# A gated linear recurrence and a gated feed-forward layer on one core: half-wide first gate units, weights read by 32 partitions, and early transfers issued by GpSimd

## The chip, the cores and the metric

The kernel runs on one core of a Trainium2 chip. A core has engines that run side by side and wait for each other by semaphores: TensorE (matrix products, with a separate step that loads the stationary operand), VectorE, ScalarE, GpSimd, and SyncE, which here only issues transfers. Transfers are carried out by 16 DMA engines. The metric is the time of one execution on the device, in microseconds; lower is better. The three timed executions of the kernel before gave 872.43, 873.46 and 875.8 us, so the time before is 873.46 us.

## The reference, cut to what matters

```python
# attention: B, H, S, D = 4, 8, 768, 48
mag = sqrt(a_re**2 + a_im**2)
scale = minimum(mag, 0.999) / (mag + 1e-06)
a = (a_re + 1j * a_im) * scale             # one complex gate per feature and step
for t in range(S):
    state = a[t] * state + outer(k[t], v[t])   # state: D x D per head, kept as re and im
    y[t] = q[t] @ state.real

# feed-forward, on x = y with heads side by side: 3072 rows of 384 features, inner width 1536
rms = sqrt(mean(x * x) + 1e-06)
xn = x / rms * rms_g
out = (silu(xn @ w_gate) * (xn @ w_val)) @ w_out
```

The three weights come as 64-bit floats and must be made 32-bit floats on the chip.

## The kernel before

The 768 steps of each of the four batches are cut into chunks of 128 rows, 24 in all. Within a chunk the recurrence is a masked product of rotated and scaled keys and queries; between chunks a state is carried. Gates are worked on in *units* of two chunks (256 rows): magnitudes, running products, arctangents, running sums of angles, sines and cosines, and then the rotation of k and q. The rotated rows are moved by transfers into the layout that TensorE needs (`kr`, `qr`).

The program is written in lanes of steps. A small scheduler (`Order`) gives each step an estimated duration and picks the next step by estimated time when the program is built; this fixes the order of the instructions on every engine. On the chip each engine goes through its own list in order.

```python
def load_gates():
    for u in range(NU):                       # NU = 12 units of UC = 2 chunks
        ...
        for name, ap in (("re", a_re), ("im", a_im)):
            aside = u == 0 and name == "im"   # ScalarE issues the first im, SyncE the rest
            yield step("ACT" if aside else "SP", 0.0 if aside else 3 * order.ISSUE, ...)

def gates():
    n1 = ND * T                               # 768 elements per partition
    ...
    for u in range(NU):
        ...                                   # squares, roots, magnitudes (ScalarE, VectorE)
        yield E("ACT", ac_us(n1), [K("tan")], lambda: act_(out=im, in_=im, func=AF.Arctan), table=["atan"])
        ...                                   # running products, running sums, sine, cosine
        for i, (o, x, f) in enumerate((("ks", "k", s), ("k", "k", y), ("qs", "q", s), ("q", "q", y))):
            ...                               # rotations: rot0 .. rot3

def move_rows():                              # moves of the rotated rows, all issued by SyncE
    ...
            def move(i, t=t, two=two):
                name, rows = ("kr", "qr")[i // 2], (1 - i % 2) * D
                ...
                for j in range(ND):
                    nc.sync.dma_start(out=two[name][rows + j * L:rows + (j + 1) * L],
                                      in_=t[("ks", "k", "qs", "q")[i]][:, j])
    ...                                       # dec, decay: the chunk's decay by way of HBM

def rows_of(ap, j):                           # how a third of a gate or value weight is read
    return ap.rearrange("(p j l) f -> j p l f", j=ND, l=32)[j]

# raw weights: 18 pieces of 0.79 MB; the first EARLY = 4 have buffers of their own,
# the others share two
def fetch():
    ...
                for j in range(ND):
                    nc.sync.dma_start(out=to[:, j], in_=rows_of(ap[:, f:f + n], j))

def narrow():                                 # 64-bit floats to 32-bit ones, four steps a piece
    for i, (to, ap, _, _) in enumerate(parts):
        ...
        yield step("ACT", 0.05 + ac_us(n), [("raw", i)], share, ends=[("share", i)])
        yield step("DVE", tt_us(n), [("raw", i), ("piece", i - 2) if i > 1 else None], shifted)
        yield step("DVE", tt_us(n), [("share", i)], signed, ends=[("both", i)])
        yield step("POOL", 1.6, [("both", i)], total, ends=[("piece", i)])

def scores():
    for n in range(N):                        # N = 24 chunks
        ...                                   # s_ps = kr.T @ qr per head (TensorE), mask (VectorE)
        ...                                   # kt_ps: keys turned (TensorE), kt copied (ScalarE)

def finish():
    ...                                       # state_ps, the carried state, y_ps

def feed_forward(groups):
    for g in groups:                          # 12 groups of two chunks
        for f in range(NF):                   # 12 tiles of the inner width
            ...                               # gv_ps: gate and value product (TensorE)
            ...                               # silu (ScalarE), times value into hT (VectorE)
        for i in range(UC):
            for part in range(2):             # out_ps: half an output each (TensorE)
                ...
```

Between `y_ps` and the feed-forward product stand the row norm: squares on ScalarE, a sum on TensorE (`ss_ps`), a power on GpSimd, a spread on TensorE, and `xT` on VectorE.

Of the kernel before, what the change touches and what calls it, by code (L numbers as in the profile page):

```python
# [28 lines left out]
P = 128  # L29
C = 128  # L30
# [15 lines left out]
class Order:  # L46
# [11 lines left out]
    RATE = 0.2  # L58

    def __init__(self):  # L60
        self.clock, self.ends, self.lanes, self.table, self.moved = {}, {}, [], None, 0.0
        self.free = {}
# [4 lines left out]
    def begin(self, step, late):  # L67
# [10 lines left out]
        return at + late, at  # L78

    def run(self):  # L80
        while self.lanes:
# [19 lines left out]
            lane[2] = None  # L101
            emit()
# [3 lines left out]
            if switch:  # L106
                self.table = more["table"][0]
            self.clock[engine] = end = at + us + switch
            if "mb" in more:
                self.moved = max(self.moved, at + 0.4) + more["mb"] / self.RATE  # L110
                end = self.moved + self.LAND
# [438 lines left out]
def fast(tc, ctx, qT, kT, v, a_re, a_im, w_gate, w_val, w_out, rms_g, out, H, bad):  # L550
# [12 lines left out]
    NU = N // UC  # L563
# [13 lines left out]
    EARLY = 4  # L577
    first = ExitStack()
    early = first.enter_context(tc.tile_pool(name="early", bufs=EARLY))
    pools = {}  # L580
# [15 lines left out]

    def columns(x, j, odd, p):


        at = 128 * p + (0, 32 + 16 * odd, 80)[j]  # L600
        return x.rearrange("p h d -> p (h d)")[:, at:at + 32]

    def rows_of(ap, j):

        return ap.rearrange("(p j l) f -> j p l f", j=ND, l=32)[j]
# [21 lines left out]
    starts = filled("starts", [P, ND, UC, C], 0.0)  # L627
# [8 lines left out]
    ends = consts.tile([P, NU, ND, UC], FP32, name="ends")  # L636
    range_ = consts.tile([P, NU], FP32, name="range_")
# [7 lines left out]
    gcol = consts.tile([P, ND], FP32, name="gcol")  # L645

# [3 lines left out]
    UN = [dict() for _ in range(NU)]  # L650
    U = [dict() for _ in range(N)]


    def load_gates():
        for u in range(NU):
            b, c = divmod(u * UC, NCH)
            t = UN[u]

            def gate(name, ap, queue, t=t, b=b, c=c):
                t[name] = prep.tile([P, ND, T], FP32, tag=name, name=name, bufs=2)  # L660
                rows = ap[b].rearrange("(h j l) s -> j l h s", j=ND, l=L)
                for j in range(ND):
                    queue.dma_start(out=t[name][:, j], in_=rows[j][:, :, c * C:c * C + T])

            for name, ap in (("re", a_re), ("im", a_im)):
                aside = u == 0 and name == "im"
                yield step("ACT" if aside else "SP", 0.0 if aside else 3 * order.ISSUE,
                           [("moved3", u - 2) if u > 1 else None],
                           lambda name=name, ap=ap, q=nc.scalar if aside else nc.sync: gate(name, ap, q),
                           mb=0.39, ends=[(name, u)])  # L670

    def load_rows():
        for u in range(NU):
            t = UN[u]

            def rows(name, ap, t=t, u=u):
                t[name] = prep.tile([P, ND, T], FP32, tag=name, name=name)
# [516 lines left out]
```

## Time and profile before

The profile follows one execution of 872.1 us.

| engine | busy us | share of the span |
|---|---|---|
| TensorE, products | 748.0 | 86% |
| TensorE, weight loads | 608.4 | 70% |
| VectorE | 414.2 | 47% |
| ScalarE | 352.4 | 40% |
| GpSimd | 57.7 | 7% |

| group of instructions | count | busy us | mean ns |
|---|---|---|---|
| up-projection, gate and value (two rows) | 1728 | 428.1 | 388 and 381 |
| output product | 576 | 194.7 | 491 |
| scores | 384 | 61.6 | 326 |
| state | 320 | 35.0 | 269 |
| VectorE, gate operation over 768 elements | 12 each | 11.4 to 13.0 | 948 to 1083 |
| ScalarE, gate operation over 768 elements | 12 each | 9.9 to 11.2 | 828 to 933 |
| GpSimd, last step of a weight's conversion | 18 | 35.8 | about 1990 |

A product of 32-bit floats is two instructions in these counts. TensorE's matmuls overlap each other, so a busy share near 100% means only that it has no gap. In the slices of the page each digit is a tenth of one fortieth of the span (21.8 us). The chain that ended last is 64% TensorE and 13% transfers. 75.24 of the 76.46 MB that are moved go through one queue, SyncE's; ScalarE's carries 0.39 MB, and no data transfer is issued by GpSimd.

### The profile page before, as it was taken

How to read it: one execution, taken by the hardware profiler on the slowest of the kernel's cores; microseconds unless marked ns; L12 is line 12 of the kernel's file. 1: busy time of each engine (PE TensorE's matmuls, PEld its weight loads, DVE VectorE, ACT ScalarE, POOL GpSimd, SP SyncE). 2: the span in 40 equal slices, each digit the busy share in tenths (PEclk: the TensorE clock that was granted, in tenths of full speed). 3: DMA queues.
4: the chain of work that ended last, by engine and by line, in shares of the span. 5: the costliest groups of instructions: out<-in, count | busy, mean ns of one | idle time of the engine just before them, and what ended most of it. 6: DMA issues, size and time to landing. Idle time of an engine off the chain costs nothing.

```text
span 872.1 us, 11793 instructions
## 1 busy us (share of the span) xinstructions
PE 748.0 (86%) x4770; PEld 608.4 (70%) x4770; DVE 414.2 (47%) x684; ACT 352.4 (40%) x544; POOL 57.7 (7%) x66
## 2 busy tenths in 40 slices
PE   0008848769788989999999999999999999999997
PEld 0007647668565778878787788877788778886784
DVE  5636537658677776765845664212211222311120
ACT  6525436546566766776743663110111111110010
POOL 2210102101121000000000000000000000000000
PEclk9999957979889999999999999999999999999999
DMA  5345544674837936666318370008400026200420
GB/s 154 102 87 145 107 91 139 100 169 99 153 97 111 146 101 95 110 123 84 82 30 111 81 108 1 0 11 110 155 0 1 1 66 189 72 1 23 159 73 22
DMA packets 98330, 76.46 MB, mean 88 GB/s; under 512 B 36828, under 2 KB 85980, under 8 KB 98268
## 3 DMA queue, kind: packets, MB, share of 16 engines
q1 hardware_dynamic: 97836, 75.24, 41.1%
q8 instruction: 39, 0.64, 0.3%
q10 hardware_dynamic: 432, 0.39, 0.2%
q14 instruction: 23, 0.19, 0.1%
HBM read 51.98 MB, written 4.76 MB: 65 GB/s over the span
## 4 chain that ended last, share of the span: by engine, by line
PE 64%; DMA 13%; DVE 5%; ACT 3%; SPq 2%; issue 1%; POOL 0%; DVEq 0%; ACTq 0%
PE gv_ps L1072 33%; PE out_ps L1096 18%; PE y_ps L996 3%; PE s_ps L927 3%; PE state_ps L967 3%; DMA dec<-ends 3%; DMA kr<-k 3%; DMA qr<-qs 2%; DMA raw<-in_w_val_dram 2%; SPq L800 1%; PE ss_ps L1019 1%; PE kt_ps L946 1%; DMA kr<-ks 1%; DMA raw<-in_w_out_dram 1%; DVE k L589 1%
## 5 line engine op out<-in xcount | busy, mean ns | idle before, releaser
L1072 PE MATMUL gv_ps<-xT,wg 128*128 128x256 f32 x864 | 216.9, 388 | 2.7 <-DVE xT L592 1.5
L1072 PE MATMUL gv_ps<-xT,wv 128*128 128x256 f32 x864 | 211.2, 381 | 1.2 <-POOL wv L885 1.2
L1096 PE MATMUL out_ps<-wo,hT 128*128 128x384 f32 x576 | 194.7, 491 | 1.4 <-POOL wo L885 1.3
L1072 PEld LDWEIGHTS gv_ps<-xT,wg 128*128 128x128 f32 x864 | 165.1, 194 | 28.3 <-issue 2.4
L1072 PEld LDWEIGHTS gv_ps<-xT,wv 128*128 128x128 f32 x864 | 165.3, 191 | 24.4 <-POOL wv L885 1.6
L589 DVE TENSOR_TENSOR hT<-gv_ps,hT 128x256 f32<-128x256 f32 x144 | 59.9, 422 | 218.3 <-ACT hT L1076 218.2
L1096 PEld LDWEIGHTS out_ps<-wo,hT 128*128 128x128 f32 x576 | 107.5, 191 | 70.8 <-POOL wo L885 2.7
L1076 ACT ACTIVATE hT<-gv_ps 128x256 f32<-128x256 f32 x144 | 54.2, 383 | 209.6 <-PE gv_ps L1072 209.2
L927 PE MATMUL s_ps<-qr,kr 96*128 96x128 f32 x384 | 61.6, 326 | 86.9 <-DMA dec<-ends 67.8
L927 PEld LDWEIGHTS s_ps<-qr,kr 96*128 96x128 f32 x384 | 57.0, 235 | 89.5 <-issue 87.6
L1029 POOL TENSOR_TENSOR rs<-ssq,mhalf 128x1 f32<-128x1 f32 x24 | 17.1, 714 | 571.3 <-DVE ssq L1024 570.4
L1105 ACT COPY ot<-out_ps 128x384 f32<-128x384 f32 x24 | 11.3, 477 | 93.0 <-PE out_ps L1096 93.0
L967 PE MATMUL state_ps<-vz,kt 128*96 128x48 f32 x320 | 35.0, 269 | 15.3 <-ACT kt L950 15.3
L967 PEld LDWEIGHTS state_ps<-vz,kt 128*96 128x96 f32 x320 | 34.4, 187 | 19.0 <-ACT kt L950 16.3
L592 DVE SCALAR_TENSOR_TENSOR xT<-y_ps,gcol,rb 128x128 f32<-128x128 f32 x72 | 20.9, 344 | 38.5 <-ACT rb L1037 25.6
L932 DVE TENSOR_TENSOR am<-s_ps,causal 128x512 f32<-128x512 f32 x48 | 32.1, 684 | 9.0 <-PE s_ps L927 8.4
L905 DVE TENSOR_REDUCE least__115<-raw 128x1 f32<-128x768 f32 x18 | 17.0, 945 | 31.0 <-DMA raw<-in_w_out_dram 16.3
L1076 ACT ACT_TABLE_LOAD x24 | 30.8, 1283 | 0.4
L950 ACT COPY kt<-kt_ps 128x384 f32<-128x384 f32 x40 | 17.5, 479 | 33.3 <-PE kt_ps L946 33.3
L996 PE MATMUL y_ps<-am,vz 128*32 128x128 f32 x768 | 29.2, 299 | 0.0
L589 DVE TENSOR_TENSOR sz<-state_ps,sz 96x384 f32<-96x384 f32 x16 | 8.8, 550 | 40.0 <-PE state_ps L967 39.9
L996 PEld LDWEIGHTS y_ps<-am,vz 128*32 128x32 f32 x768 | 21.9, 119 | 4.9 <-issue 3.3
(97 smaller groups left out, 731.0 us busy)
## 6 DMA issues: line engine op xcount, KB each, us to landing
raw<-in_w_out_dram SPq DMA_DIRECT2D x12, 768.0 KB
re<-in_a_re_dram SPq DMA_DIRECT2D x36, 128.0 KB
k<-in_k_dram SPq DMA_DIRECT2D x24, 192.0 KB
q<-in_q_dram SPq DMA_DIRECT2D x24, 192.0 KB
vz<-in_v_dram SPq DMA_DIRECT2D x24, 192.0 KB
raw<-in_w_gate_dram SPq DMA_DIRECT2D x18, 256.0 KB
raw<-in_w_val_dram SPq DMA_DIRECT2D x18, 256.0 KB
kr<-ks SPq DMA_DIRECT2D x36, 128.0 KB
```

Of the source, the lines that this page charges most:

```text
L589: nc.vector.tensor_tensor(out=o, in0=x, in1=y, op=op)
L592: nc.vector.scalar_tensor_tensor(out=o, in0=x, scalar=c, in1=y, op0=op0, op1=op1, **kw)
L905: nc.vector.tensor_reduce(out=least_[:, i:i + 1], in_=words(raws.pop(i))[1].bitcast(FP32), axis=mybir.AxisListType.X, op=ALU.min, apply_ab ...
L927: nc.tensor.matmul(u["s_ps"][a][:, h], lhsT=u["k"][:, a * HH + h], rhs=u["q"][:, a * HH + h], start=True, stop=True)
L932: nc.vector.tensor_tensor(out=u["am"][a], in0=u["s_ps"][a], op=ALU.mult, in1=causal.unsqueeze(1).to_broadcast([C, HH, C]))
L950: nc.scalar.copy(out=u["kt"][a], in_=u["kt_ps"][a])
L967: nc.tensor.matmul(u["st_ps"][:, h], lhsT=u["kt"][h // HH][:, h % HH], rhs=u["v"][:, h, 0:D], start=True, stop=True)
L996: nc.tensor.matmul(u["y_ps"][32 * p:32 * (p + 1), j], lhsT=columns(left, j, odd, p), rhs=right(h), start=side == 0 and i == 0, stop=side = ...
L1029: nc.gpsimd.tensor_tensor(out=u["rs"], in0=u["ssq"], in1=mhalf, op=ALU.pow)
L1072: nc.tensor.matmul(ps[:, i], lhsT=w_[:, f * P // FW, d, cols], rhs=t["xT"][:, d], start=d == 0, stop=d == ND - 1)
L1076: nc.scalar.activation(out=t["hT"][:, f], in_=t["gv", f][:, 0], func=AF.Silu)
L1096: nc.tensor.matmul(t["o_ps", i], lhsT=t["hT"][:, f, i * C:(i + 1) * C], rhs=wo[:, f], start=f == 0, stop=f == NF - 1)
```

## The change: what it does and what it is for

1. **Half-wide first units.** The first unit of two chunks is split into two units of one chunk. Their operations cover 384 elements instead of 768, so that the first chunk's rows can be rotated before the second chunk's are done.
2. **Where raw weights land.** The four buffers for early raw weights are gone. The first four pieces land in the buffers `hT` of the feed-forward layer, which are not needed until later, and the others in two buffers `raw2` and in one half of `hT`.
3. **By 32 partitions.** A raw gate or value weight is read in four transfers of 32 partitions with three runs each, instead of three transfers of 128 partitions. The gain `rms_g` is read in the same manner.
4. **Who issues.** GpSimd issues the first six raw weights and, for the first two units, the moves of `qs` and `q`. ScalarE issues `im` for both half units.
5. **Fillers.** Where the scheduler expects TensorE to stand idle before a product that starts a stage, it places products of two constants (`ident`, `causal`) into the tile that the stage overwrites anyway. They are to keep TensorE's clock up.
6. **The scheduler.** It knows a slow state of TensorE, two transfer queues, and that GpSimd's sum holds VectorE; conversions of weights are held back until the first rotations are placed.

The listed order of the instructions changes accordingly: chunks 0 and 1 are interleaved on VectorE and ScalarE without a weight between them; TensorE does all twelve up-projection tiles of group 0 and one half output before chunk 2's scores, where before six tiles stood; ten fillers stand before the first scores and ten before chunk 2's.

```diff
+    units = [(0, 1), (1, 1)] + [(n, UC) for n in range(2, N, UC)]
+    NU = len(units)
...
+    def busy(ps):
+        n = ps.shape[1] // C
+        for _ in range(int((order.gap - 0.3) / (n * 0.215))):
+            nc.tensor.matmul(ps, lhsT=ident[:, 0:ps.shape[0]], start=True, stop=True,
+                             rhs=causal.unsqueeze(1).to_broadcast([C, n, C]))
...
-    def rows_of(ap, j):
-        return ap.rearrange("(p j l) f -> j p l f", j=ND, l=32)[j]
+    def rows_of(ap, p):
+        return ap.rearrange("(p j l) f -> p l j f", j=ND, l=32)[p]
...
+    hT = [consts.tile([P, NF, T], FP32, name="hT%d" % i) for i in range(2)]
+    raw2 = [consts.tile([P, ND, 2 * FW], I32, name="raw%d" % i) for i in range(2)]
...
-                aside = u == 0 and name == "im"
+                aside = u < 2 and name == "im"
...
             def move(...):
+                queue = nc.gpsimd if u < 2 and i > 1 else nc.sync
...
-                    nc.sync.dma_start(out=two[name][rows + j * L:rows + (j + 1) * L],
+                    queue.dma_start(out=two[name][rows + j * L:rows + (j + 1) * L],
...
+    EARLY = 6
+    def room(i):
+        two = (0, 1) if i < 2 else (2, 3) if i < 2 * NW and i % 4 > 1 else (4, 5)
...
+            aside = i < EARLY
+            queue = nc.gpsimd if aside else nc.sync
...
-                for j in range(ND):
-                    nc.sync.dma_start(out=to[:, j], in_=rows_of(ap[:, f:f + n], j))
+                for p in range(H // 2):
+                    queue.dma_start(out=to[32 * p:32 * (p + 1)], in_=rows_of(ap[:, f:f + n], p))
...
-            yield step("POOL", 1.6, [("both", i)], total, ends=[("piece", i)])
+            more = dict(late=lambda i=i: (0.05 if i < 2 * NW else 0.3) if ("rot", 1) in order.ends else LATE)
+            yield step("POOL", 2.3, [("both", i)], total, ends=[("piece", i)], holds=("DVE", 1.2))
...
             def pairs(u=u):
                 for a in range(2):
                     u["s_ps"].append(ps_a.tile([C, HH, C], FP32, tag="a", name="s_ps"))
+                    if a == 0:
+                        busy(flat(u["s_ps"][a]))
...
-    order.lane(gates(), 0.1)
+    order.lane(gates([0]), 0.05)
+    order.lane(gates(range(1, NU)), 0.1)
```

## The prediction, made before the changed kernel had run

> **What bounds the kernel now.** I read the page's forty slices first, then cut the span into stages where the slices change, then asked who TensorE waits for, then read the transfers of the first stage. The slices (TensorE's busy tenths, its granted clock, the DMA engines, GB/s):
>
> ```profile
> PE   0008848769788989999999999999999999999997
> PEclk9999957979889999999999999999999999999999
> DMA  5345544674837936666318370008400026200420
> ```
>
> TensorE does nothing in three slices, is ragged and partly at a low clock up to about slice 14, and is full afterwards. The table by stage (TensorE busy, weight loads, VectorE, ScalarE, GpSimd, then clock, DMA share, GB/s):
>
> ```profile
> 0.00:63.60 63.60, 0.00 (x0) 0.03 (x1) 32.93 (x39) 29.13 (x35) 14.03 (x28) 1.00 0.48 118
> 63.60:116.00 52.40, 37.58 (x264) 33.25 (x264) 29.87 (x51) 27.68 (x39) 6.53 (x5) 0.89 0.52 114
> 116.00:174.00 58.00, 44.68 (x321) 39.84 (x321) 35.92 (x57) 27.18 (x39) 9.02 (x6) 0.76 0.51 116
> 174.00:310.00 136.00, 112.11 (x847) 90.45 (x848) 98.52 (x149) 85.39 (x119) 18.53 (x12) 0.88 0.66 124
> 310.00:865.50 555.50, 553.51 (x3341) 444.83 (x3340) 216.78 (x392) 182.49 (x314) 9.60 (x15) 1.00 0.33 70
> ```
>
> From 310 us on TensorE is 99.6% busy at full clock: nothing can be won there except by arriving with more work done. Before 310 us it stands still for 63.6 us, then loses 246.4 - 194.4 = 52 us to gaps, and runs part of the rest at the low clock. What it waits for, up to 310 us (total, times, longest):
>
> ```profile
> PE s_ps L927 <- DMA dec<-ends: 67.8, 3, 63.6
> PE s_ps L927 <- DMA qr<-q: 17.3, 3, 9.2
> PE state_ps L967 <- ACT kt L950: 15.3, 3, 7.2
> ```
>
> These are rotated rows that arrive late, and a copy on ScalarE. The chain behind that copy leads to a raw weight: before the state product at 129.15 stand a transfer of 9.37 us (118.37) and the conversion behind it in ScalarE's order. Why are transfers slow? SyncE's issues, and the DMA from 20 to 40 us:
>
> ```profile
> 20.85 8.22 SPq L853 DMA_DIRECT2D raw<-in_w_gate_dram  x3
> 29.12 7.62 SPq L853 DMA_DIRECT2D raw<-in_w_val_dram  x3
> 36.84 3.76 SPq L800 DMA_DIRECT2D kr<-ks  x3
> ...
> DMA  2222222222222222222222222222222222222223
> GB/s 106 98 98 102 106 98 102 98 98 98 98 98 102 102 98 98 98 102 98 98 98 102 98 98 98 98 106 98 98 98 98 98 102 98 98 98 98 102 98 117
> ```
>
> A quarter of the engines works, at a constant 98 GB/s; issues that take 1.9 us for three elsewhere take 8. The first rotated rows were ready on VectorE at 31.6 us but were issued at 36.84, and the last landed only at 63.6.
>
> **The Trainium skill.** "DMA: Bandwidth & Descriptors", section "Why a DMA increments its semaphore by 16 and not by 1", says that the number of engines is the largest k up to 16 dividing the slowest dimension of both patterns. Gate and value weights are read as p=4, l=32: k is 4, and 98 GB/s on a share of 0.26 agrees. With l=32 outermost k is 16. "TensorE: Matmul & The Clock Gate", Part 1, says that the array's clock halves after an idle window of some 3.4 us and comes back after as long a busy one. The trace agrees: the first eight score products take 3.75 us at 63.6 and 1.85 us at 320.71. "SBUF — State Buffer", "Who interferes with whom", says that a VectorE instruction with two SBUF inputs blocks against a GpSimd one that reads SBUF. Agrees: a product of 0.95 us took 2.46 at 27.36 beside GpSimd's weight sum (26.54 to 29.0). The DMA page's "Latency and other measured facts" gives GpSimd's transfers about 1 us to the first byte; no transfer in this trace is issued there, so this is the figure I know least.
>
> **TensorE's work, which stays.** Warm durations from the chain: an up-projection tile 2.59 us (276 instructions in 59.57), half an output 3.87 (84 in 27.09), scores 1.85, transposes 0.66, state 1.32, y 1.89 with a state and 0.90 without, sums 0.66, spread 0.22. Work: 144 x 2.59 = 373.0; 48 x 3.87 = 185.8; 24 x 1.85 = 44.4; 20 x 0.66 = 13.2; 20 x 1.32 = 26.4; 20 x 1.89 + 4 x 0.90 = 41.4; 24 x 0.88 = 21.1. Sum 705. The old span closes: 63.6 start + 705 + 52 gaps up to 310 + 2 later + 43 low clock (748.0 busy - 705) + 6.6 tail = 872.
>
> **Step 1: the start, 63.6 to about 36 us.** Half-wide operations: VectorE's rate in the trace is one 768-wide operation per 0.87 us (12.25, 13.12, 13.99); 384 fewer elements at 960 per us give 0.47. ScalarE goes from 0.74 to about 0.42. In the changed order chunks 0 and 1 interleave on both engines and no weight stands between them. Working the listed order through: loads land at 5.2; ScalarE is held until 7.1 because it issues chunk 1's loads itself (three times 0.65); the common arctangents by 17.3; scans and sums of chunk 0 by 18.2; turns 20.8; sine and cosine (with two table loads of 1.28) by 24; the four rotations of chunk 0 end at 25.4 to 26.9, of chunk 1 at 30.3 to 31.8. A move took 5.16 us where nothing stood ahead (293.52), plus 1.9 us to issue: kr at about 33. qr goes through GpSimd behind 24 weight transfers. Early data are about 2.8 MB of gates and rows and 4.7 MB of weights; at the 246 GB/s of 10 to 15 us this takes 30 us, so GpSimd is through with them when the rotations end. First scores at about 36.
>
> **Step 2: up to chunk 2's scores, about 114 us.** From the first scores to the first up-projection took 24.6 us (63.6 to 88.2); the same chain of two chunks remains, so it starts at 60.6. All twelve tiles of group 0 follow: 31.1 us, to 91.7. Before, SyncE's four-engine transfers set the pace of the weights (six tiles by 107 us); now a piece of 0.79 MB needs about 3.2 us at 246 GB/s, and twelve conversions cost VectorE 12 x 1.33 = 16 us plus about 1.2 each of lock with GpSimd. This just keeps pace. But the changed order puts the last 12 us of unit 2's gates behind the last tile's product on VectorE, and behind three table loads on ScalarE; then rotations (4 x 0.9) and moves (7): chunk 2's scores at 91.7 + 22.5 = 114. By then TensorE has done 31.1 + 12.6 (attention of chunks 0 and 1) + 3.9 (a first half output) = 47.5 us of warm work in 78: a loss of 30.5. The old kernel came to these scores at 116.06 with 28 us done. The clock time hardly moves; the work done before it does.
>
> **Step 3: from there to full load.** Fifteen of eighteen weight pieces are done, against six. Unit 3's gates need about 31 us of VectorE and as much of ScalarE per 59 us of TensorE, so from unit 4 on rows are early, and waits such as 7.24 us at 191.94 go. I leave 5 us for the state copies of chunks 2 and 3, 5 for unit 3's rows, 8 for short waits and low clock: 18.
>
> **Step 4: the fillers.** A 512-wide one is 0.86 us warm (3.87/6 per 384). The ten ahead of the first scores depend only on constants: they run at about 3 us and are over long before those scores, so they warm nothing. The ten ahead of chunk 2's scores sit in a gap of some 20 us and save perhaps 2. None lies on the path.
>
> Sum: 36 + 705 + 30.5 + 18 + 6.6 = 796; the reported time was 1.4 us above the span, so 797.5; I say 800.
>
> **Rivals.** (a) GpSimd's issue takes the place of the DMA: at 1.5 us each, 24 transfers end near 43 us, the moves of qr come after, and the weight sums after them: start about 48, everything in steps 1 and 2 shifts by 10 to 15: 812. For it: GpSimd is one in-order queue for weights, moves and sums. Against it: only 14 us busy of the first 63.6. (b) VectorE becomes the early bound: conversions, gates and locks packed into 35 to 90 us stall group 0's tiles, chunk 2 comes at 125 to 130: again 812 to 820. VectorE's 32.93 of 63.6 speaks against it, its sharing with GpSimd for it. (c) The early gain is absorbed because unit 2's rows bind at 116 anyway and the same waits return: only 15 us gained, 858. Against it: those waits end in slow raw weights, whose cause goes. (d) Everything is early, loss only 30: 778.
>
> **Range and chances.** Centre 800; 776 to 834 holds (a), (b) and (d). Slower would need a start past 100 us or late weights all along. Faster by over 2% (below 856) 0.92, within 0.06, slower 0.02.
>
> **What would show it.** Right: first scores at 33 to 42 us; all 16 DMA engines in the weight transfers and no plateau at 98 GB/s; a first-tile time near 60; a gap before chunk 2's scores near 110; full load from about 150; work from there to the end unchanged. Wrong: GpSimd transfers spaced well over 1 us, qr as the releaser of the first scores far behind kr, up-projections waiting on GpSimd's sums, or gaps of over 4 us after 150 us.

## The result: 834.3 us, a gain of 4.6% where 8.4% was predicted

| | before | after |
|---|---|---|
| time, median | 874.4 us | 834.3 us (831.1 to 837.0) |
| ratio, 95% interval | | 0.954 [0.949, 0.959] |
| profiled span | 872.1 us | 829.0 us |
| TensorE, VectorE, ScalarE, GpSimd busy | 748.0, 414.2, 352.4, 57.7 us | 761.3, 428.7, 360.8, 79.6 us |

The change is faster, as predicted; the size is missed: 834.3 lies just above the range of 776 to 834. (Ratios leave disturbed executions out, medians do not, so the two can differ by some tenths of a per cent.)

The slices of the page after, with the same rows as before (TensorE's busy tenths, granted clock, DMA engines):

```profile
PE   5079967989998999999999999999999999999996
PEclk9556987989998999999999999999999999999999
DMA  8929637562647276554635470045100106200510
```

TensorE's first digit is now work on fillers; real work begins in the third slice instead of the fourth, and the full row of nines begins in the 14th instead of the 16th. The table by stage (the columns are those of the table before: TensorE, weight loads, VectorE, ScalarE, GpSimd, then clock, DMA share, GB/s):

```profile
0.00:43.10 43.10, 10.74 (x20) 4.50 (x20) 25.18 (x55) 26.11 (x45) 24.64 (x61) 0.69 0.96 197
43.10:78.50 35.40, 30.01 (x200) 24.78 (x201) 18.14 (x27) 9.81 (x17) 13.01 (x9) 0.55 0.61 130
78.50:138.40 59.90, 47.35 (x177) 34.31 (x175) 56.97 (x62) 35.19 (x47) 23.04 (x12) 0.92 0.63 137
138.40:177.00 38.60, 36.44 (x298) 29.03 (x298) 28.89 (x46) 24.87 (x36) 4.35 (x3) 0.94 0.63 118
177.00:310.00 133.00, 126.90 (x971) 106.61 (x972) 91.47 (x153) 86.11 (x121) 4.58 (x6) 0.95 0.49 93
310.00:822.40 512.40, 509.81 (x3158) 410.68 (x3156) 208.07 (x372) 178.70 (x301) 10.00 (x14) 1.00 0.33 74
```

The stages end at the first scores (43.1), the first up-projection tile (78.5), chunk 2's scores (138.4) and unit 3's (177). After 310 us TensorE is 99.5% busy at full clock, as before. Two rows stand out: in the first the DMA engines are busy 96% of the time, and in the third VectorE is busy 57 of 60 us. What TensorE waits for up to 320 us (total, times, longest):

```profile
PE s_ps L1014 <- DMA kr<-k: 33.0, 2, 29.8
PE s_ps L1014 <- DMA dec<-ends: 8.8, 2, 4.8
PE out_ps L1184 <- POOL wo L968: 7.8, 2, 5.0
```

The waits on copies of keys (15.3 us before) are gone; rotated rows still open the list. I use one measure below. **Loss** at a moment is the time elapsed minus the warm work that TensorE has done by then, counted from the instructions in the trace at the prediction's durations (fillers count as nothing). The work of a whole run comes to 705 us by this count, in every run. The loss can be read at each milestone:

| run | first scores | first tile | chunk 2's scores | loss at first tile | loss at chunk 2 | loss at the last product |
|---|---|---|---|---|---|---|
| before | 63.6 | 88.2 | 116.1 | 76.0 | 88.3 | 160.2 |
| predicted | 36 | 60.6 | 114 | 48.0 | 66.5 | 84.5 |
| after | 43.2 | 78.6 | 138.4 | 66.3 | 91.2 | 116.6 |

So the changed kernel reaches chunk 2's scores with slightly more loss than the old one (91.2 against 88.3). It wins behind that point: it loses 25 us there, the old one 72.

### The profile page after: what moved, and what is told of

Its sections match the earlier page's. It is cut to its first block, busy times and chain, and to the rows that moved or that the text cites. A ratio compares the mean times of both kernels' runs of the same rounds, so it can differ in the third digit from the quotient of the medians.

```text
span 829.0 us, 12028 instructions
## 1 busy us (share of the span) xinstructions
PE 761.3 (92%) x4820; PEld 609.9 (74%) x4820; DVE 428.7 (52%) x709; ACT 360.8 (44%) x565; POOL 79.6 (10%) x103
## 4 chain that ended last, share of the span: by engine, by line
PE 76%; DMA 8%; DVE 7%; ACT 3%; SPq 2%; issue 2%; POOL 1%; DVEq 0%; ACTq 0%; POOLq 0%
PE gv_ps L1160 39%; PE out_ps L1184 20%; PE s_ps L1014 5%; PE y_ps L1087 5%; PE state_ps L1057 3%; SPq L861 2%; DMA hT<-in_w_gate_dram 2%; DMA qr<-q 2%; PE ss_ps L1110 2%; DMA qr<-qs 1%; PE kt_ps L1035 1%; DMA raw<-in_w_gate_dram 1%; DMA dec<-ends 1%; PE ss_ps L1123 1%; DMA raw<-in_w_out_dram 1%
## 5 line engine op out<-in xcount | busy, mean ns | idle before, releaser
L1160 PE MATMUL gv_ps<-xT,wg 128*128 128x256 f32 x864 | 213.8, 384 | 0.2
L1160 PEld LDWEIGHTS gv_ps<-xT,wv 128*128 128x128 f32 x864 | 164.6, 190 | 22.5
L1014 PE MATMUL s_ps<-qr,kr 96*128 96x128 f32 x384 | 57.0, 310 | 45.3 <-DMA kr<-k 33.0
L1014 PEld LDWEIGHTS s_ps<-qr,kr 96*128 96x128 f32 x384 | 53.0, 221 | 48.7 <-issue 48.6
L1057 PEld LDWEIGHTS state_ps<-vz,kt 128*96 128x96 f32 x320 | 32.2, 176 | 1.6 <-issue 0.7
L1057 PE MATMUL state_ps<-vz,kt 128*96 128x48 f32 x320 | 32.1, 257 | 0.0
L1128 ACT COPY rb<-ss_ps 128x128 f32<-128x128 f32 x24 | 6.3, 264 | 59.1 <-PE ss_ps L1123 59.1
L1110 PEld LDWEIGHTS ss_ps<-ones,sq 128*128 128x128 f32 x144 | 20.3, 202 | 8.5 <-ACT sq L1105 5.0
```

Of the source, the lines that this page charges most:

```text
L1014: nc.tensor.matmul(u["s_ps"][a][:, h], lhsT=u["k"][:, a * HH + h], rhs=u["q"][:, a * HH + h], start=True, stop=True)
L1057: nc.tensor.matmul(u["st_ps"][:, h], lhsT=u["kt"][h // HH][:, h % HH], rhs=u["v"][:, h, 0:D], start=True, stop=True)
L1110: nc.tensor.matmul(u["ss_ps"][:, 0:1], lhsT=u["sq"][:, d], rhs=ones, start=d == 0, stop=d == ND - 1)
L1160: nc.tensor.matmul(ps[:, i], lhsT=w_[:, f * P // FW, d, cols], rhs=t["xT"][:, d], start=d == 0, stop=d == ND - 1)
```

## Experiments

Two theories follow from this. **Layout**: reading raw weights on all DMA engines carries nearly the whole gain, by making weights early. **Parts**: half units, GpSimd's issues, fillers and the new order each bring some of it. For the missing 33 us: (i) the start is held by crowded transfers, (ii) VectorE holds chunk 2 back, or (iii) the listed order does. Where a step, a need or an estimated duration was altered, the scheduler listed the order of all engines anew; a run then tests the edit together with its new order. The order stayed as it was in the two layout runs, in the run without fillers and in the one named "the same order".

### Which part carries the gain

**Layout alone**, in the kernel before:

```diff
-                for j in range(ND):
-                    nc.sync.dma_start(out=to[:, j], in_=rows_of(ap[:, f:f + n], j))
+                for p in range(H // 2):
+                    nc.sync.dma_start(out=to[32 * p:32 * (p + 1)], in_=rows_32(ap[:, f:f + n], p))
```

> The kernel before, with one thing changed: raw gate and value weights are read by 32 partitions, four transfers a piece, still issued by SyncE, order of all instructions as before. Theory (slow four-engine transfers were the root of the early waits): no plateau at 98 GB/s, SyncE's issues of a piece about 2.5 us, first scores at about 52 to 56 us instead of 63.6, waits behind raw weights between 116 and 240 us mostly gone, total 845 to 856 us. Rival (the gain of the whole change comes from the half units and the new order): total 868 to 876 us.

Measured: 838.4 us, ratio 0.957 [0.955, 0.959], more than the theory had expected. First scores 44.7, first tile 72.6, chunk 2's scores 92.0. One line of layout brings 36 of the 40 us, with every engine's order unchanged. Two thirds of it stand already at chunk 2's scores: the loss is 60.3 at the first tile (before: 76.0), 64.2 at chunk 2 (88.3) and 124.9 at the end (160.2). So the layout helps the start as well as the later weights.

**Layout undone**, all other parts kept:

```diff
-                for p in range(H // 2):
-                    queue.dma_start(out=to[32 * p:32 * (p + 1)], in_=rows_of(ap[:, f:f + n], p))
+                for j in range(ND):
+                    queue.dma_start(out=to[:, j], in_=rows_4(ap[:, f:f + n], j))
```

> The changed kernel with one part undone: gate and value weights are read again in three transfers of 128 partitions (four partition groups outermost) instead of four of 32 partitions; half units, GpSimd's issues, the new order and the fillers stay. Theory (the layout is nearly the whole gain): 850 to 880 us; the transfers run on a quarter of the engines at 98 GB/s, the 9.4 MB of gate and value weights then last to about 100 us, first scores come early (33 to 38 us, because nothing crowds the moves), but the up-projections of the first group wait for weights. Rival (half units, GpSimd's issues and order are worth 10 us or more by themselves): 835 to 850 us.

Measured: 865.8 us, 0.988 [0.986, 0.991]; first scores 50.0, first tile 87.1, chunk 2's scores 170.1. The time is as the layout theory has it, the early start that I expected is not: with the transfers of GpSimd's queue the engines are 95% busy up to 50 us all the same, at 171 GB/s. That several slow transfers run side by side there, with the query rows behind them, is my reading of it. Later, with SyncE's weights alone, the plateau is back (the last twenty of forty slices from 50 to 110 us read 98 to 102 GB/s). This is what the Trainium skill says in "DMA: Bandwidth & Descriptors", section "Why a DMA increments its semaphore by 16 and not by 1": the sizes of the outermost dimensions, not the bytes, decide how many engines work. The trace agrees: from 80 to 110 us, with the four partition groups outermost, the engines' busy share is 0.26 at 100 GB/s; with 32 partitions outermost the changed kernel's first stage has 0.96 at 197 GB/s.

**Fillers out, the same order:**

```diff
     def busy(ps):
-        n = ps.shape[1] // C
-        for _ in range(int((order.gap - 0.3) / (n * 0.215))):
-            nc.tensor.matmul(ps, lhsT=ident[:, 0:ps.shape[0]], start=True, stop=True, ...)
+        return
```

> The changed kernel in exactly the same order, without the filler products. Theory (fillers lie in gaps and hardly act): 832 to 837 us; the six before the first up-projection go (they end some 2 us after its input is there), but that product then starts at the low clock and loses about 1.5 us. Rival (fillers keep the clock up, as intended): 840 to 848 us, with the first up-projections and chunk 2's products at half clock for several us longer.

Measured: 835.3 us, 0.951 [0.947, 0.954]. The interval overlaps that of the changed kernel: the fillers make no difference that can be told. Those ahead of chunk 2's scores end at 133.7 us, 4.8 us before these scores, which then take 3.76 us; without fillers they take 3.75.

**Half units undone:**

```diff
-    units = [(0, 1), (1, 1)] + [(n, UC) for n in range(2, N, UC)]
+    units = [(n, UC) for n in range(0, N, UC)]
...
```

> The changed kernel with one part undone: the first two chunks are one full-width unit again; the reading by 32 partitions, GpSimd's issues of early transfers, two conversion lanes and fillers stay. (A half output also waits for the conversion of each of its weight pieces, which the changed kernel's order gives anyway.) Theory (the start is bound by the crowded transfers, not by the gates): first scores at 42 to 50 us and 828 to 840 us, no difference to the changed kernel that can be told. Rival (the half units do bring chunk 0 forward): first scores at 50 to 56 us and 842 to 850 us.

Measured: 837.7 us, 0.958 [0.955, 0.960]: no difference that can be told. The first scores come 4 us later (47.1), but chunk 1's follow after 4.7 us instead of 8.8, and the first tile comes 10 us earlier (68.5).

**GpSimd's issues undone:**

```diff
-                queue = nc.gpsimd if u < 2 and i > 1 else nc.sync
+                queue = nc.sync
...
-            queue = nc.gpsimd if aside else nc.sync
+            queue = nc.sync
...
```

> The changed kernel with one part undone: the early weights and the moves of the first two chunks' query rows are issued on SyncE again instead of on GpSimd; layout, half units, order and fillers stay (a half output also waits for each of its pieces' conversions). Theory (the transfers' bytes, not who issues them, set the start): first scores at 41 to 47 us, 830 to 838 us. Rival (SyncE's queue of issues, 3 us a piece, holds the moves back): first scores at 48 us or later, 840 us or more.

Measured: 828.6 us, 0.947 [0.945, 0.950]; first scores at 43.2, to the tenth as with GpSimd, though the first tile came later (85.4). Who issues does not matter to the first scores; if anything GpSimd's part costs a little.

So "parts" has fallen as long as the layout is there: layout alone gives 0.957, everything together 0.954, and the intervals meet. Without the layout the other parts bring some 1% (0.988 [0.986, 0.991]), so the gains do not add up. Two parts were not undone alone: where raw weights land, and what the scheduler knows.

### What holds the start

The DMA of the changed kernel from 0 to 40 us (busy tenths and GB/s in forty slices, the software queue, then issues with size and median time to landing):

```profile
DMA  0046595899999999999999999999999999999999
GB/s 0 0 129 176 150 308 152 255 262 218 215 239 227 222 238 230 230 226 232 227 233 227 226 161 236 211 228 188 218 239 226 227 221 233 199 222 165 138 205 235
...
q0 software_dynamic: 1722, 5.11, 58.2%
...
k<-in_k_dram SPq DMA_DIRECT2D x2, 192.0 KB, 11.9
...
kr<-ks SPq DMA_DIRECT2D x3, 64.0 KB, 9.5
```

From 8 us on the engines are busy throughout, at 219 GB/s to the end of the window: 8.17 MB in all, of them 5.11 MB through GpSimd's queue. The rotated rows of chunk 0 were ready at 27.1 to 28.8 us, near the predicted 25.4 to 26.9. A 64 KB move then took 9.5 us to land, and issuing the first three took 5.12 us instead of the predicted 1.9. Chunk 1's rotations should have ended at 31.8; they ended at 40.0, because VectorE stood for its k and q rows, which came late out of the same crowd:

```profile
34.30 0.56 DVE L612 TENSOR_TENSOR k<-k,r 128x384 f32<-128x384 f32 x1 [3.74 <-DMA k<-in_k_dram]
37.26 0.56 DVE L612 TENSOR_TENSOR q<-q,p 128x384 f32<-128x384 f32 x1 [2.41 <-DMA q<-in_q_dram]
```

**Early pieces held:** pieces 3 to 6 of the weights only after chunk 1's rotations.

```diff
-                       [("re", 0) if aside else ("moved3", 0), ...],
+                       [("re", 0) if i < 2 else ("rot3", 1) if aside else ("moved3", 0), ...],
```

> The changed kernel with GpSimd's raw weights 3 to 6 held back until the second chunk's rotations (two early pieces instead of six before the moves); the scheduler orders anew. Theory (early weights fill all 16 DMA engines and delay the rows): chunk 1's k and q land before 22 us instead of 34 to 37, first scores at 33 to 37 us instead of 43.2, second chunk's scores before 42; total 822 to 830 if the later weights still keep up. Rival 1 (GpSimd's own issue is what is late): first scores stay at 41 or more. Rival 2 (weights become late instead): first scores early, but gaps in group 0's up-projections, total 834 or more.

Measured: 828.1 us, 0.947 [0.945, 0.950]; first scores 37.7, just behind the expected range, chunk 1's at 48.6 instead of before 42, first tile 68.1. In this run's order one half output reads one weight piece before the last step of its conversion. The next run adds the need that a half output waits for each of its pieces (the runs with half units or GpSimd's issues undone, and all later ones of the changed kernel with held pieces, have it too, with one like it for group 1's first tile):

```diff
-                    yield step("PE", NF * pe_us(DM), [("h", g, fs[-1]), ("piece", 2 * NW + fs[-1] // 2)],
+                    yield step("PE", NF * pe_us(DM), [("h", g, fs[-1])] + [("piece", 2 * NW + f // 2) for f in fs],
```

> The changed kernel, with weight pieces 3 to 6 not issued until chunk 1's rows are rotated, as in the run before that held them, but now every half output waits for the conversion of each weight piece that it reads. Theory (crowded transfers cost the start 5 us, and it is kept to the end): first scores at 36 to 39 us, 824 to 831 us. Rival (the shift is used up by chunk 2's rows): 832 to 836 us.

Measured: 822.2 us, 0.940 [0.937, 0.944]; first scores 39.8, first tile 70.5, chunk 2's scores 131.0, loss at the end 106.7. This is the fastest kernel that leaves nothing out: 12 us below the changed one.

**Decays written early as well.** SyncE writes a decay to HBM, waits until it has landed, and reads it back; in the changed kernel it stood from 37.25 to 45.03 us for this, with chunk 1's moves behind (SyncE's issues):

```profile
37.25 0.39 SPq L873 DMA_DIRECT2D dec<-ends  x1
45.03 1.26 SPq L876 DMA_DIRECT2D decay<-dec  x2
46.38 1.86 SPq L861 DMA_DIRECT2D kr<-ks  x3
```

In this run, besides the held pieces, the write goes ahead of the moves:

```diff
+            yield step("SP", 0.5, [("p", u)], spill, mb=0.02, queue="rows", ends=[("spilt", u)])
             for i in range(4):
                 ...                                   # moves
-            yield step("SP", 1.3, [("p", u)], decays, mb=0.02, then=2.5, ...)
+            yield step("SP", 0.8, [("spilt", u)], decays, mb=0.02, ...)
```

> The kernel with pieces 3 to 6 held (822.2 us), and in addition the decays are written to DRAM as soon as they are known, ahead of the moves, so that SyncE no longer stands between their writing and their reading (6 to 10 us twice in the first 60 us and 7 us before chunk 2). Theory (SyncE's stand held back chunk 1's rows and the weights behind them): SyncE issues chunk 1's moves by 38 us, chunk 1's scores follow chunk 0's within 7 us, chunk 2's scores 5 us earlier, 815 to 820 us. Rival (something else ends last: GpSimd's query rows, the weight sums): 821 to 825 us.

TensorE's timeline in this run (start, duration, instruction, wait ahead):

```profile
36.08 3.75 PE L1019 MATMUL s_ps<-qr,kr 96*128 96x128 f32 x16 [22.52 <-DMA qr<-q]
...
61.63 1.46 PE L1165 MATMUL gv_ps<-xT,wg 128*128 128x256 f32 x6
...
66.81 2.74 PE L644 MATMUL gv_ps<-causal,ident 128*128 128x512 f32 x6
```

First scores at 36.1 and first tile at 61.6: the two milestones that I had predicted at 36 and 60.6. Theory (i) holds for the start: in the seven runs of the changed kernel with held pieces, those below included, the first scores came at 36.1 to 40.1 us, in the seven with early pieces at 42.4 to 50.0. Writing the decays early is not shown to matter there: of the seven, the three that do it have 36.1, 38.3 and 40.1. And chunk 1's scores still followed after 9.3 us, not within 7. The time is 828.6 us, 0.945 [0.941, 0.949], not the expected 815 to 820: the loss is 17 us smaller than in the changed kernel at the first tile (49.4 against 66.3), 16.5 smaller at chunk 2 (74.7 against 91.2) and only 4 at the end (112.4 against 116.6). An early start is mostly used up later.

**Held pieces in the simple kernel** (layout alone, pieces from 2 on after chunk 0's and 1's moves):

```diff
-                                    ("moved3", 0) if i >= EARLY else None]
+                                    ("moved3", 0) if i >= 2 else None]
```

> The kernel before with the reading by 32 partitions, and in addition weight pieces 2 and up are issued only after chunk 0's and 1's rows are moved (before: from piece 4 on). Theory (moves queue behind weights on the engines): first scores from 44.7 to 36 to 40 us, and the time from 838 to 830 to 835 us. Rival (the early weights are needed as much as the rows, chunk 2's rows and the first tiles then wait for weights): first scores early all the same, time 836 to 845 us.

Measured: 863.1 us, 0.983 [0.978, 0.987], first scores 45.1. Both expectations of the first scores failed. Its DMA from 0 to 46 us:

```profile
DMA  0087645768899999999600000017999999999900
GB/s 0 4 258 228 191 107 143 200 205 258 231 287 211 203 164 217 230 232 232 139 23 0 0 0 0 0 33 197 132 118 118 120 117 119 120 116 117 64 0 0
...
kr<-ks SPq DMA_DIRECT2D x3, 128.0 KB, 3.8
kr<-k SPq DMA_DIRECT2D x3, 128.0 KB, 5.4
qr<-qs SPq DMA_DIRECT2D x3, 128.0 KB, 6.6
qr<-q SPq DMA_DIRECT2D x3, 128.0 KB, 7.9
```

No weight is in the way, and the four moves still need 13 us: they fill all engines and pass only 118 GB/s, and each lands later than the one before. The unit's 1.57 MB (12 transfers of 128 KB) at 118 GB/s make 13.3 us. A half unit has half of it, so an estimate of what half units can save at the start is 6.7 us; the pair of runs above, with new lists, showed 4. The 25 us lost against layout alone come later (loss at chunk 2 68.0 against 64.2, at the end 149.6 against 124.9): half outputs wait for the last step of their weights as late as 221 and 263 us (up to 6.9 us). How much of the 25 us is this, and how much the new list, is not shown.

### What holds chunk 2 and the time behind it

VectorE is 95% busy from 78.5 to 138.4 us, and part of that is GpSimd's doing. The clearest case stands ahead of this stage (start, duration, VectorE's and then GpSimd's instructions of the changed kernel):

```profile
42.65 5.33 DVE L612 TENSOR_TENSOR s<-s,w 128x768 f32<-128x768 f32 x1
```

```profile
43.55 1.83 POOL L968 TENSOR_TENSOR wg<-t,wg 128x768 int32<-128x768 int32 x1
45.34 1.81 POOL L968 TENSOR_TENSOR wv<-t,wv 128x768 int32<-128x768 int32 x1
```

A VectorE sum of 0.95 us takes 5.33 beside two sums of GpSimd. This is the case that "SBUF — State Buffer", section "Who interferes with whom", of the Trainium skill describes, and the trace agrees. Over the twelve sums of the stage from 78.5 to 138.4 us the lengthened instructions (shifts of 1.2 to 2.2 us instead of 0.55, products of 1.8 to 2.6 instead of 0.95) add up to some 16 us.

**The last conversion step on VectorE:**

```diff
             def total(...):
-                nc.gpsimd.tensor_tensor(out=to, in0=part["t"], in1=to, op=ALU.add)
+                stt(to, part["t"], 0x7FFFFFFF, to, ALU.bitwise_and, ALU.bitwise_xor)
```

> The changed kernel with the last step of a weight's conversion on VectorE (a bitwise operation of one more 0.95 us) instead of a sum on GpSimd; the low word is scaled by 7.4/8 so that it has no carry. The scheduler orders anew. Theory (VectorE is the bound from 78 to 138 us, and GpSimd's sums block it by about 1.5 us each, 12 of them there): no VectorE operation over 1.2 us besides scans, chunk 2's scores at 122 to 128 us instead of 138.5, total 815 to 823. Rival (the listed order and ScalarE's table loads set the pace of unit 2, VectorE only looks full): chunk 2's scores at 134 or later, total 830 to 836.

Measured: 829.2 us, 0.947 [0.945, 0.949]. (The low word is scaled by 7.4/8, so part of the last bits' rounding is left out.) The first tile comes at 66.0 us, 12.5 earlier, chunk 2's scores at 135.0, only 3.5 earlier. Where the other 9 us went is in part seen: the slowing of 16 us was exchanged for twelve operations of 0.95 us, 11.4 us, which leaves 4.6; and the early tiles ran into weights that had not landed (TensorE waited 8.1 us for a product of VectorE, which in its order stood behind a piece that was 9.7 us late).

With held pieces:

> The kernel with pieces 3 to 6 held (822.2 us), and the weights' last step as a bitwise operation on VectorE instead of a sum on GpSimd. (The low word is scaled by 7.4/8, so it leaves out part of the last bits' rounding.) If the slowed VectorE (5 us beside two sums) and the waits for GpSimd's sums (15.7 us of TensorE) cost time of their own: 815 to 819 us, waits of half outputs for weight sums below 6 us. If they only stand where another wait would: 820 to 826 us, as without it 829 against 834.

Measured: 828.3 us, 0.945 [0.942, 0.948]: no gain over held pieces alone. With held pieces and early decays:

> All three together: pieces 3 to 6 held, decays written early, last weight step on VectorE. If their gains add: 808 to 815 us. If they share one wait before chunk 2's scores: 816 to 822 us.

Measured: 839.6 us, 0.959 [0.957, 0.960]. Edits that gained over the changed kernel (the VectorE step, and held pieces with and without early decays) gain nothing when put together. Its chunk 2 comes at 130.0, 8 us later than without the VectorE step, and its loss at the end is 127.0.

**Low words left out, the same order.** The low word is the lower half of a 64-bit weight. ScalarE's and GpSimd's steps of the conversion go; the weights are cut to 20 bits of fraction.

```diff
-                nc.scalar.activation(out=to, in_=part["lo"].bitcast(U32), func=AF.Copy, ...)
...
-                nc.vector.tensor_scalar(..., scalar1=3, scalar2=None, op0=ALU.logical_shift_left)
+                nc.vector.tensor_scalar(..., scalar1=3, scalar2=0x3FFFFFFF,
+                                        op0=ALU.logical_shift_left, op1=ALU.bitwise_and)
...
-                stt(to, part["hi"], -2 ** 31, to, ALU.bitwise_and, ALU.bitwise_or)
+                stt(to, part["hi"], -2 ** 31, part["t"], ALU.bitwise_and, ALU.bitwise_or)
...
-                nc.gpsimd.tensor_tensor(out=to, in0=part["t"], in1=to, op=ALU.add)
+                return
```

> The changed kernel in the same order on every engine, with the weights' low words left out: ScalarE's conversion and GpSimd's sum are gone, VectorE keeps a shift with a mask (0.55 us) and the sign (0.95). The weights are cut to 20 bits of fraction, so part of the computation is left out. Theory (VectorE and its slowing beside GpSimd set chunk 2): the 57 us of VectorE between first tile and chunk 2's scores fall by the 16 us of slowing, chunk 2's scores come 14 to 20 us after their 138.4, at 118 to 124, and the time falls by 8 us or more, to 820 to 826. Rival (transfers and their order on SyncE set it): chunk 2's scores at 130 or later, 829 to 834 us.

The stage from the first tile to chunk 2's scores of this run, cut at 125 us (same columns as the table by stage):

```profile
78.50:125.00 46.50, 41.98 (x167) 32.74 (x166) 33.66 (x52) 19.01 (x29) 0.00 (x0) 0.95 0.55 147
```

VectorE now has 28% of air, GpSimd does nothing, and chunk 2's scores still come at 136.2, 2 us earlier. So theory (ii) does not explain chunk 2. What holds it is read from the chain of waits (start, duration, what), here of the same run:

```profile
77.31 34.03 PE gv_ps L1158 x144
...
111.36 0.39 ACT hT L1162
...
111.77 0.42 DVE hT L612
112.20 1.95 DVE re L816 x3
...
121.28 0.96 DVE ks L612
...
124.19 0.96 DVE q L612
...
130.42 5.65 DMA dec<-ends
```

All twelve tiles of group 0, then the last product into `hT` on VectorE, then in VectorE's order the last running sums and the rotations of unit 2, and its moves. The view puts the last piece down to the decay's write, but this cannot be it. The scores read only `kr` and `qr`, and they began at 136.18, before SyncE could read the decay back:

```profile
128.52 1.85 SPq L861 DMA_DIRECT2D qr<-q  x3
130.42 0.60 SPq L873 DMA_DIRECT2D dec<-ends  x1
137.88 0.82 SPq L876 DMA_DIRECT2D decay<-dec  x2
```

So the chain ends with the last moves of query rows. The listed order ties chunk 2 to the last tile of group 0. From the last tile's end to chunk 2's scores it takes 28.8 us in the changed kernel (109.6 to 138.4) and still 25.0 here (111.2 to 136.2): the low words' load is 4 us of it, the chain in this order the rest. This is (iii), read from the trace: no run moved unit 2's gates alone. In the run with SyncE's issues, whose list has more of these gates ahead of the last tile, the same stretch took 17.3 us (118.6 to 135.9). The late first tile has the same kind of cause. VectorE's timeline in this run ahead of the first tile:

```profile
74.23 0.56 DVE L959 TENSOR_SCALAR t<-hT 128x768 int32<-128x768 int32 x1 [7.11 <-DMA hT<-in_w_gate_dram]
...
76.91 0.86 DVE L615 SCALAR_TENSOR_TENSOR xT<-y_ps,gcol,rb 128x128 f32<-128x128 f32 x3
```

`xT`, which the first tile needs, is listed behind the conversion of a weight piece whose transfer SyncE issued only at 65.7 us. In the changed kernel the same wait is 2.12 us.

The whole time did fall, to 825.9 us, 0.943 [0.941, 0.944]: 8 us, of which 2 stand at chunk 2. So the low words' load costs time behind chunk 2 as well; there it is not one long wait.

**The same with held pieces:**

> The kernel with pieces 3 to 6 held (822.2 us), low words left out as in the run beside it. Theory (conversion): 805 to 814 us. Rival (order of transfers): 819 to 823 us.

Measured: 817.1 us, 0.933 [0.931, 0.935], between the two expectations. TensorE and SyncE have the order of the run with held pieces, so this load is worth 5 us there. **With early decays and a new list:**

> Pieces held, decays written early, low words left out, and the order of all engines listed anew with these costs. If the predicted 800 us failed only by the crowded start and by the conversion's load: 796 to 806 us. If loads of later chunks and waits in order take it: 812 to 825 us.

Measured: ratio 0.932 [0.927, 0.937], some 816 us (all executions: 812.9 to 825.9, median 822.9). The predicted 800 us do not come back by lifting the start and the conversion; the rival's range, that of later waits, holds.

**Low words left out in the simple kernel** (before plus layout):

> The kernel before with the reading by 32 partitions (838.4 us) and low words left out, listed anew. It spent 57 us of loss after chunk 2's scores, more than any other. Theory (conversion load): 815 to 825 us. Rival (its full-width start and order): 830 to 838 us.

Measured: 810.9 us, 0.924 [0.922, 0.927], the fastest of all runs. First scores 42.0, first tile 70.6, chunk 2's scores 88.4; no tile order ties chunk 2 there. The loss is 60.6 at chunk 2 and 100.6 at the end; with full weights it was 64.2 and 124.9. So 24 us are gained, 21 of them behind chunk 2. This run has a new list as well, and what the low words' load is worth with the list kept was measured only in the changed kernel (8 and 5 us); how the 24 us divide is not shown. Its stages from chunk 2's scores on:

```profile
88.40:130.00 41.60, 32.73 (x298) 28.63 (x297) 31.36 (x54) 27.28 (x39) 1.34 (x2) 0.91 0.82 143
130.00:310.00 180.00, 167.11 (x1257) 136.60 (x1257) 136.73 (x215) 118.25 (x164) 7.47 (x6) 0.96 0.70 132
310.00:806.00 496.00, 493.92 (x2956) 396.35 (x2954) 176.49 (x328) 144.15 (x261) 9.05 (x14) 1.00 0.30 66
```

The longest waits of the layout run between 92 and 310 us:

```profile
PE state_ps L970 <- ACT kt L953: 12.6, 3, 5.9
PE s_ps L930 <- DMA qr<-q: 6.5, 3, 2.6
PE s_ps L930 <- DMA dec<-ends: 5.9, 2, 4.6
```

The copies of keys, which stand behind ScalarE's conversions in its order, are the largest; without low words (88 to 310 us) this wait is not in the list any more, `qr<-q` has 3.8 us and `dec<-ends` 9.7.

**Slowing or load?** The last step on VectorE in the simple kernel:

> The kernel before with the reading by 32 partitions (838.4 us), and the weights' last step as a bitwise operation on VectorE instead of a sum on GpSimd; order listed anew. (The low word is scaled by 7.4/8, so it leaves out part of the last bits' rounding.) If the slowing beside GpSimd is what cost the simple kernel: 815 to 825 us. If it is the load of the conversion (18 operations of 0.95 us are added): 832 to 842 us.

Measured: 854.7 us, 0.980 [0.975, 0.984]. GpSimd no longer slows VectorE, 18 operations of 0.95 us are added, and it loses 16 us against layout alone; even the "load" expectation was too mild. The list is new here too, so these 16 us are not the load's alone. Half outputs wait for weight conversions as late as 257 us (7.3 us). **Early decays on the fastest kernel:**

> The simple kernel with the new layout and low words left out (810.9 us), and in addition the decays are written to DRAM as soon as they are known, ahead of the moves. SyncE stood 5.6 us and 8.2 us between writing and reading before chunks 0 and 2. Theory (this stand is on the path): first scores from 42 to 38 us, chunk 2's scores 5 us earlier, 801 to 807 us. Rival (query rows and VectorE end last anyway): 808 to 813 us.

Measured: 822.2 us, 0.939 [0.933, 0.946], 11 us slower than without. First scores came at 43.6, not at 38. Chunk 2's scores came 2 us earlier (86.3), but with 23 us of work done against 28, and chunk 3's scores 7 us later (97.8 against 90.8). The edit itself only moves a write of 3 KB; that the new list of all engines costs more than it gains is the likely reading, not tested apart.

## Why the prediction was right in direction and wrong in size

| term | predicted | measured |
|---|---|---|
| first scores | 36 | 43.2 |
| first scores to first tile | 24.6 | 35.4 |
| twelve tiles of group 0 | 31.1 | 31.1 |
| from there to chunk 2's scores | 22.5 | 28.8 |
| loss behind them | 18 | 25.4 |
| warm work | 705 | 705.4 |
| after the last product | 6.6 | 7.0 |

The four excesses, 7.2 + 10.8 + 6.3 + 7.4 = 31.7 us, and 1.1 us of small terms (0.3 us less work done at chunk 2's scores, 0.4 each in the last two rows) bring the predicted sum of 796 to 829; the span was 829.0. What was right is that the layout makes the weights early and that the old waits behind them go; what failed is the price of the start and of the chain from there to chunk 2's scores.

**Step 1 failed in the price of a move and in its sum of bytes.** "At the 246 GB/s of 10 to 15 us this takes 30 us, so GpSimd is through with them when the rotations end": GpSimd did issue its last weight at 27.57, but a weight's transfer took 8.5 us to land, the rate was 219 GB/s, the first 8 us were not full, and the moves themselves were left out of the bytes. Chunk 0's rotations were right within 2 us, chunk 1's were 8 us late. A move was taken at the 5.16 us of an idle stretch and 1.9 us of issue; it took 9.5 behind bulk weights, and 5.1 us of issue. The held-piece runs show that the crowd is the cause: with it lifted, the first scores come at 36.1 to 40.1 us.

**Step 2 failed at "the same chain of two chunks remains, so it starts at 60.6".** The chain measured in the old kernel has both chunks' rows in one unit; with half units chunk 1's rows come on their own. Its scores came 8.8 us after chunk 0's instead of 4.8, because its rotations were late and its moves stood behind SyncE's wait for the decay; with whole units they came after 4.7 us and the chain took 21.4. `xT` stood behind a late weight piece (2.1 us). And the products of this chain ran long: 24.6 us of them, without fillers, against 20.1 before, at a granted clock of 0.55 against 0.92. In the run with held pieces and early decays the chain took 25.5 us; but chunk 1's scores were as late there (9.3 us), and it was the products that were short (16.3 us at 0.84), so it is partly luck that the predicted 60.6 was nearly met there. "This just keeps pace" was right for the tiles. The end of step 2, unit 2's gates behind the last tile's product, was the right mechanism and 6 us too small. Gates and rotations took 17.6 us instead of 15.6 (13.9 with low words left out). The moves took 11.2 instead of 7: SyncE issues four of them one after the other, 1.9 us each, so that the last one began 3.5 us after its rows were ready (127.3), and the scores began 6.4 us after its last transfer was issued (132.0).

**Step 3** was 7 us off, about as much as executions of the changed kernel differ among themselves (831.1 to 837.0). It rested on a right reading: weights are ready early, and the old waits on key copies go. Of the 25.4 us, 10.5 are gaps and 15 products slower than warm ones; step 3 had 8 for short waits and low clock together. **Step 4** was right that the fillers lie off the path; the 2 us that it hoped for ahead of chunk 2 were not seen.

**Rivals.** (a) predicted a late start for a wrong reason: GpSimd issued a transfer in 0.55 us. From the tenth on they stood 1.1 us apart, each behind the landing of an earlier one, and the start is the same with SyncE. (b) had nearly the right moment for chunk 2 (125 to 130 against 138.4) and VectorE at 95%, but the run in the same order with VectorE relieved shows that the low words' load adds only 2 to 4 us there. (c), absorption, was put aside too soon: 17 us gained at the first tile end as 4.

Still open: why lists of nearly the same work in the changed kernel lose from 23 us (held pieces) to 44 us (all three edits) behind chunk 2. The runs show where single ones wait, not a rule that would have foretold it.

## What to carry to other kernels

Undo and do alone each part of a compound change: here one line of layout gave 36 of 40 us, and with it in place half units, GpSimd's issues and fillers gave nothing that could be told. Where engines work through lists in order, an early milestone is worth only what the lists behind it allow, so price the chain that follows (last tile, gates, and each move's turn in the queue of issues) and not the milestone. Count the bytes of small critical transfers into the same budget as the bulk, and hold back bulk that is not needed yet.

## What the runs showed that I had not expected

- Moves of rotated rows in 128 KB transfers fill all DMA engines at 118 GB/s with nothing beside them; bulk weights, gates and moves together ran at 219. The engines' busy share alone does not tell the rate.
- Quarter-engine weight transfers on GpSimd's queue left the engines 95% busy up to 50 us (171 GB/s, with the other loads); the plateau at 98 GB/s came where SyncE alone issued such transfers.
- Moving a write of 3 KB, or the sums from one engine to another, changed the time by anything from 5 us less to 16 us more, each time with a new list of instructions. Leaving the low words out altogether, in the same list, was worth 5 and 8 us.
